# Other beginnings for the operands that TensorE streams, and two VectorE steps in another form

## The chip, the cores and the metric

One NeuronCore of a Trainium2 chip runs the kernel. The metric is the device time of one execution in microseconds; the time before is a median of 3 runs, and one more execution was profiled. Engines are named as in the profile: PE (TensorE matmul), PEld (its weight loads), DVE (VectorE), ACT (ScalarE), POOL (GpSimd), SP (SyncE, which issues the DMAs).

## The reference

Four batches of 12,416 rows of 128 go through an induced set attention with 32 inducing points, and the result through a gated feed-forward layer of 1536.

```python
def mab(q, kv):
    s = scale * (q @ kv.transpose(0, 2, 1))
    s = s - s.max(-1, keepdims=True)
    a = np.exp(s)
    a /= a.sum(-1, keepdims=True) + 1e-09
    return a @ kv
h = mab(I, x)
return mab(x, h).astype(np.float32)
...
g = x @ w_gate
silu = g * (1.0 / (1.0 + np.exp(-g)))
val = x @ w_val
return (silu * val @ w_out).astype(np.float32)
```

## The kernel before

The second attention is never written out. Its values `h` (32 rows) are multiplied into the two input weights of the feed-forward layer, which gives the tile `tw` for each batch. The attention weights of the rows, transposed and split into a rounded part and its rest (`a_hi`, `a_lo`, in the type fp32r), are copied by DMA into a tile `stack`, so that `tw` times `stack` is at once the gate and the value of the layer.

A batch has 25 column tiles: `COLS` lists one of the first four blocks (512 columns), then twelve of 16 blocks each (512 columns, numbers 1 to 12) and twelve of 15 blocks (480 columns, numbers 13 to 24). For each column tile the loop runs over 12 slices of the 1536 hidden units; one pass of it is a slot, 300 slots a batch. In a slot `front` issues two matmuls that stream `stack` (L668 gate, L669 value), ACT applies silu (L671), DVE multiplies (L676). One slot later `split` (from L679) makes `h_hi`, the product rounded to fp32r (L685, ACT or DVE), and `h_lo`, its rest (L687, POOL, or DVE for three of twelve slices). Five to ten slots after that (`SKEW`, `HI`), `back` issues three matmuls into one accumulator: `h_hi` with `wo_lo` (L701), `h_hi` with `wo_hi` (L702), `h_lo` with `wo_hi` (L703). After twelve slices DVE copies the accumulator out (L710) and SP stores it. The first column tile of the first batch is done in plain fp32 (L699) instead.

The operand that streams through PE is the second one here, of 512 or 480 columns; the weights are 128 columns of `tw`, `wo_hi` or `wo_lo`, loaded beside the matmul before. `stack` has three buffers, `h_hi` eleven, `h_lo` ten (`BF`, `NST`), each of 512 words a partition; gate and value share six PSUM buffers, two a tile.

The attention of the next batch is laid between the slots by due times (`plan`, `post`). For each group of blocks `post` issues: `sum2` (DVE: a sum, L441, and the addition of 1e-9, L442), `rec2` (DVE, L445), `norm2` (POOL, L449), `aT` (DVE transpose, L453), `a_hi` (DVE copy that rounds, L457; one of them, in the first batch, on ACT), `a_lo` (POOL, L462), and later `spread`, the DMAs into `stack`. Three short columns are made at the start on POOL: `odd`, `half`; a small tile `z` serves a short cut of the first batch only. `proj_c` (L397) is a correction matmul of the first batch that streams `tw` itself with the weights `below`; L385 is an fp32 matmul that makes `tw`.

The schedule is by hand (`tc.manual_schedule`), so the order of the code is the order on each engine. Pools lie in SBUF in the order in which they are opened.

Of the kernel before, what the change touches and what calls it, by code (L numbers as in the profile page):

```python
# [9 lines left out]
F32 = mybir.dt.float32  # L10
F32R = mybir.dt.float32r
AF = mybir.ActivationFunctionType
ALU = mybir.AluOpType
# [4 lines left out]
B, N, C, M, DFF = 4, 12416, 128, 32, 1536  # L18
P = 128
NG = 4  # L20
# [10 lines left out]
FC = [4, 16, 16, 16, 15, 15, 15]  # L31
FC0 = starts(FC)
NF = len(FC)
W = 32 * max(CH)
WF = 32 * max(FC)
NT = DFF // P
SCALE = 1.0 / math.sqrt(C)


COLS = [(0, 0)] + [(q, j) for q in range(1, NF) for j in range(NG)]  # L40
SLOTS = len(COLS) * NT
NXT = 4
# [66 lines left out]
def induced_set_attention_then_swiglu(ctx: ExitStack, tc: tile.TileContext, xt, xn, ind, wgv, wo, out):  # L109
    nc = tc.nc  # L110

    const = ctx.enter_context(tc.tile_pool(name="const", bufs=1))
    xtp = ctx.enter_context(tc.tile_pool(name="xtp", bufs=NXT))
    att = ctx.enter_context(tc.tile_pool(name="att", bufs=2))
    sgl = ctx.enter_context(tc.tile_pool(name="sgl", bufs=1))
    eTp = ctx.enter_context(tc.tile_pool(name="eTp", bufs=4))
    one = ctx.enter_context(tc.tile_pool(name="one", bufs=1))
    stp = ctx.enter_context(tc.tile_pool(name="stp", bufs=NST))
# [13 lines left out]
    group = const.tile([P, NG], F32, name="group")  # L132
    nc.vector.tensor_reduce(out=group, in_=ident.rearrange("p (j m) -> p j m", m=M), op=ALU.add, axis=AX.X)

    odd = const.tile([P, 1], F32, name="odd")
    nc.gpsimd.memset(odd, 0.0)
    for j in (1, 3):
        nc.gpsimd.memset(odd[32 * j:32 * j + 32, :], -1.0)


    half = const.tile([P, 1], F32, name="half")
    nc.gpsimd.memset(half[:64, :], 0.0)
    nc.gpsimd.memset(half[64:, :], -1.0)

    indT = const.tile([P, M], F32, name="indT")
    nc.sync.dma_start(out=indT, in_=ind)
# [15 lines left out]
    class Piece:  # L162
# [28 lines left out]

        def lo(self):
            nc.gpsimd.tensor_sub(out=wo_lo[:, self.cs], in0=self.w, in1=wo_hi[:, self.cs].bitcast(F32))

    class Batch:
        pass

    def attention(b, one, xn0=None, xt0=None):

        st = Batch()  # L200
# [216 lines left out]
        def sl2(b0, b1):  # L417
            return st.s2[:, b0:b1, :]
# [19 lines left out]
        def sum2(q):  # L438
            st.sm[q] = att.tile([P, 16], F32, name="sm")
            sm = st.sm[q][:, :FC[q]]  # L440
            nc.vector.tensor_reduce(out=sm, in_=sl2(*fblocks(q)), op=ALU.add, axis=AX.X)  # L441
            nc.vector.tensor_scalar(out=sm, in0=sm, scalar1=1e-9, scalar2=None, op0=ALU.add)  # L442

        def rec2(q):
            nc.vector.reciprocal(out=st.sm[q][:, :FC[q]], in_=st.sm[q][:, :FC[q]])  # L445
# [5 lines left out]
        def aT(q):  # L451
            st.at[q] = sgl.tile([P, WF], F32, name="aT")
            nc.vector.transpose(out=st.at[q][:, :32 * FC[q]], in_=sl2(*fblocks(q)).rearrange("p t m -> p (t m)"))  # L453

        def a_hi(q, eng=nc.vector.tensor_copy):
            st.ah[q] = sgl.tile([P, WF], F32R, name="a_hi")
            eng(out=st.ah[q][:, :32 * FC[q]], in_=st.at[q][:, :32 * FC[q]])  # L457

        def a_lo(q, eng):
            st.al[q] = sgl.tile([P, WF], F32R, name="a_lo")  # L460
            n = 32 * FC[q]
            eng.tensor_sub(out=st.al[q][:, :n], in0=st.at[q][:, :n], in1=st.ah[q][:, :n].bitcast(F32))  # L462

        def stack(u):
            if u not in st.stack:
                st.stack[u] = stp.tile([P, WF], F32R, name="stack")
            return st.stack[u]

        def spread(u):
# [19 lines left out]
            nc.vector.tensor_reduce(out=st.zm, in_=st.zps[:, :M * FC[0]].rearrange("p (t m) -> p t m", m=M), op=ALU.max, axis=AX.X)  # L489

        def z2():
            st.z = att.tile([P, FC[0], M], F32, name="z")
            nc.vector.tensor_sub(out=st.z, in0=st.zps[:, :M * FC[0]].rearrange("p (t m) -> p t m", m=M),
                                 in1=st.zm.unsqueeze(2).broadcast_to([P, FC[0], M]))

# [46 lines left out]
    def plan(st, p):  # L542
# [6 lines left out]
        def clear(slot):  # L549

            while slot % NT in p["TABU"]:
                slot += 1
# [50 lines left out]
    with tc.tile_pool(name="xt0", bufs=NCH - NXT) as xt0, tc.tile_pool(name="xn0", bufs=NCH - NXN) as xn0, tc.tile_pool(name="wtmp", bufs=1) as wtmp:  # L603
# [20 lines left out]
        def run(token):  # L624
# [17 lines left out]
            at=f["aT"], ah=lambda q, e=0: f["a_hi"](q, dve_act[e]),  # L642
# [8 lines left out]
    hip = ctx.enter_context(tc.tile_pool(name="hip", bufs=BF[2]))  # L651
    lop = ctx.enter_context(tc.tile_pool(name="lop", bufs=BF[3]))
# [5 lines left out]
    def front(st, b, c, t):  # L658
        u = Tile()
        q, j = COLS[c]  # L660
        u.b, u.q, u.j, u.t = b, q, j, t
        n = u.n = WF if q == 0 else 32 * FC[q]

        u.whole = b == 0 and c == 0
        rhs = st.stack[c][:, :n]
        u.g = ps_gv.tile([P, 512], F32, name="gv")
        u.v = ps_gv.tile([P, 512], F32, name="gv")
        nc.tensor.matmul(out=u.g[:, :n], lhsT=st.w[:, wcol(0, t)], rhs=rhs, start=True, stop=True)  # L668
        nc.tensor.matmul(out=u.v[:, :n], lhsT=st.w[:, wcol(1, t)], rhs=rhs, start=True, stop=True)  # L669
        s = sip.tile([P, WF], F32, name="silu")  # L670
        nc.scalar.activation(out=s[:, :n], in_=u.g[:, :n], func=AF.Silu)  # L671
        if u.whole:
            u.h = hip.tile([P, WF], F32, name="h_hi")
        else:
            u.h = u.v if t in DVE_TILES else hp.tile([P, WF], F32, name="h")
        nc.vector.tensor_mul(out=u.h[:, :n], in0=u.v[:, :n], in1=s[:, :n])  # L676
        return u

    def split(u):  # L679
        if u.whole:  # L680
            return
        n = u.n
        u.hi = hip.tile([P, WF], F32R, name="h_hi")
        u.lo = lop.tile([P, WF], F32R, name="h_lo")
        (nc.vector.tensor_copy if u.cast_dve else nc.scalar.copy)(out=u.hi[:, :n], in_=u.h[:, :n])  # L685
        eng = nc.vector if u.t in DVE_TILES or u.last else nc.gpsimd
        eng.tensor_sub(out=u.lo[:, :n], in0=u.h[:, :n], in1=u.hi[:, :n].bitcast(F32))  # L687
# [28 lines left out]
    for b in range(B):  # L716
# [12 lines left out]
        for slot in range(SLOTS):  # L729
            c, t = slot // NT, slot % NT  # L730
            u = front(cur, b, c, t)
# [62 lines left out]
```

## Time and profile before

| what | us |
|---|---|
| median of 3 runs | 1499.35 |
| lowest and highest of them | 1498.7, 1502.27 |
| the profiled execution | 1499.66 |
| its span, first to last instruction | 1497.6 |
| PE busy | 1475.7 |
| ACT, DVE, POOL busy | 1283.6, 1214.6, 1208.5 |

The profile is of one execution. The share of busy time says which engine has no room left; the chain of waits says what set the end; the table by stretch tells stages apart; the timeline gives single starts, to 0.01 us. A matmul's recorded length is longer than the distance to the next one's start, since matmuls are pipelined, so rates are read from starts.

### The profile page before, as it was taken

How to read it: one execution, taken by the hardware profiler on the slowest of the kernel's cores; microseconds unless marked ns; L12 is line 12 of the kernel's file. 1: busy time of each engine (PE TensorE's matmuls, PEld its weight loads, DVE VectorE, ACT ScalarE, POOL GpSimd, SP SyncE). 2: the span in 40 equal slices, each digit the busy share in tenths (PEclk: the TensorE clock that was granted, in tenths of full speed). 3: DMA queues.
4: the chain of work that ended last, by engine and by line, in shares of the span. 5: the costliest groups of instructions: out<-in, count | busy, mean ns of one | idle time of the engine just before them, and what ended most of it. 6: DMA issues, size and time to landing. Idle time of an engine off the chain costs nothing.

```text
span 1497.6 us, 24960 instructions
## 1 busy us (share of the span) xinstructions
PE 1475.7 (99%) x7465; PEld 1166.2 (78%) x7465; DVE 1214.6 (81%) x2083; ACT 1283.6 (86%) x2389; POOL 1208.5 (81%) x995
## 2 busy tenths in 40 slices
PE   8899999999999999999999999999999999999999
PEld 5576777788887776788887777678888887888887
DVE  6788778878888778788888878878878878878877
ACT  5787888789898887889989888789898898898897
POOL 1588767878898778788888877978889888888887
PEclk9999999999999999999999999999999999999999
DMA  9026322221133333121114324221111111111110
GB/s 369 23 94 187 135 96 94 79 61 56 40 109 120 122 125 112 46 67 37 40 44 131 125 87 156 78 69 48 41 40 35 38 41 41 33 41 39 41 40 20
DMA packets 50822, 119.80 MB, mean 80 GB/s; under 512 B 11392, under 2 KB 28288, under 8 KB 50688
## 3 DMA queue, kind: packets, MB, share of 16 engines
q1 hardware_dynamic: 50688, 118.22, 24.6%
q8 instruction: 59, 0.97, 0.3%
q14 instruction: 75, 0.61, 0.1%
HBM read 62.87 MB, written 25.43 MB: 59 GB/s over the span
## 4 chain that ended last, share of the span: by engine, by line
PE 87%; POOL 2%; ACT 2%; DVE 1%; issue 1%; DVEq 0%; ACTq 0%; POOLq 0%
PE o L701 17%; PE o L703 17%; PE o L702 16%; PE gv L668 16%; PE gv L669 16%; PE o L257 2%; POOL h_lo L687 2%; PE o L305 1%; ACT h_hi L685 1%; ACT silu L671 1%; POOL s_all L449 1%; DVE h L676 1%; PE gv L406 0%; ACT s_all L289 0%; DVE ob L710 0%
## 5 line engine op out<-in xcount | busy, mean ns | idle before, releaser
L687 POOL TENSOR_TENSOR h_lo<-h,h_hi 128x512 fp32r<-128x512 f32 (+1 forms) x890 | 1109.5, 1270 | 238.8 <-ACT h_hi L685 186.9
L671 ACT ACTIVATE silu<-gv 128x512 f32<-128x512 f32 (+1 forms) x1200 | 704.4, 588 | 127.0 <-PE gv L668 89.6
L676 DVE TENSOR_TENSOR h<-gv,silu 128x512 f32<-128x512 f32 (+1 forms) x891 | 594.3, 668 | 206.8 <-ACT silu L671 162.3
L685 ACT CAST h_hi<-h 128x512 fp32r<-128x512 f32 (+1 forms) x788 | 475.5, 603 | 54.0 <-DVE h L676 47.6
L668 PE MATMUL gv<-stack,tw 128*128 128x512 f32 (+1 forms) x1200 | 469.3, 391 | 1.3 <-ACT h_hi L685 0.8
L701 PE MATMUL o<-h_hi,wo_lo 128*128 128x512 f32 (+1 forms) x1188 | 464.4, 391 | 3.8 <-DVE ob L710 2.1
L703 PE MATMUL o<-h_lo,wo_hi 128*128 128x512 f32 (+1 forms) x1188 | 463.2, 390 | 0.6
L669 PE MATMUL gv<-stack,tw 128*128 128x512 f32 (+1 forms) x1200 | 461.8, 385 | 1.8 <-DVE h L676 0.6
L702 PE MATMUL o<-h_hi,wo_hi 128*128 128x512 f32 (+1 forms) x1188 | 458.5, 386 | 0.0
L701 PEld LDWEIGHTS o<-h_hi,wo_lo 128*128 128x128 f32 x1188 | 223.0, 188 | 81.9 <-issue 33.9
L669 PEld LDWEIGHTS gv<-stack,tw 128*128 128x128 f32 x1200 | 225.2, 188 | 53.9 <-ACT silu L671 4.8
L668 PEld LDWEIGHTS gv<-stack,tw 128*128 128x128 f32 x1200 | 225.7, 188 | 50.2 <-issue 3.8
L703 PEld LDWEIGHTS o<-h_lo,wo_hi 128*128 128x128 f32 x1188 | 222.4, 187 | 52.6 <-POOL h_lo L687 12.1
L702 PEld LDWEIGHTS o<-h_hi,wo_hi 128*128 128x128 f32 x1188 | 223.2, 188 | 36.8
L676 DVE TENSOR_TENSOR gv<-gv,silu 128x512 f32<-128x512 f32 (+1 forms) x297 | 201.7, 679 | 46.4 <-ACT silu L671 40.7
L687 DVE TENSOR_TENSOR h_lo<-gv,h_hi 128x512 fp32r<-128x512 f32 (+1 forms) x297 | 197.3, 664 | 1.0
L685 ACT CAST h_hi<-gv 128x512 fp32r<-128x512 f32 (+1 forms) x294 | 167.9, 571 | 4.8 <-DVE gv L676 2.5
L710 DVE COPY ob<-o 128x512 f32<-128x512 f32 (+1 forms) x100 | 66.3, 663 | 1.4 <-PE o L703 1.4
L685 DVE CAST h_hi<-h 128x512 fp32r<-128x512 f32 (+1 forms) x103 | 46.1, 448 | 0.0
L462 POOL TENSOR_TENSOR a_lo<-aT,a_hi 128x512 fp32r<-128x512 f32 (+2 forms) x27 | 36.2, 1340 | 1.5 <-ACT a_hi L457 1.5
L433 POOL TENSOR_TENSOR s_all<-s_all,mx 128x448 f32<-128x448 f32 (+3 forms) x28 | 26.9, 961 | 0.7 <-DVE mx L429 0.7
L449 POOL TENSOR_TENSOR s_all<-s_all,sm 128x512 f32<-128x512 f32 (+2 forms) x27 | 25.9, 958 | 0.4 <-DVE sm L445 0.4
(159 smaller groups left out, 497.4 us busy)
## 6 DMA issues: line engine op xcount, KB each, us to landing
xt_sb<-xt SPq DMA_DIRECT2D x32, 896.0 KB, 5.1
xn_sb<-xn SPq DMA_DIRECT2D x18, 896.0 KB, 6.2
out<-ob SPq DMA_DIRECT2D x52, 256.0 KB, 2.0
out<-ob SPq DMA_DIRECT2D x48, 240.0 KB, 2.0
stack<-a_hi SPq DMA_DIRECT2D x96, 64.0 KB, 2.0
stack<-a_lo SPq DMA_DIRECT2D x96, 64.0 KB, 2.0
stack<-a_hi SPq DMA_DIRECT2D x96, 60.0 KB, 2.0
stack<-a_lo SPq DMA_DIRECT2D x96, 60.0 KB, 2.0
```

What stands on the lines that cost most here:

```text
L449: eng.tensor_mul(out=a, in0=a, in1=st.sm[q][:, :FC[q]].unsqueeze(2).broadcast_to([P, FC[q], M]))
L462: eng.tensor_sub(out=st.al[q][:, :n], in0=st.at[q][:, :n], in1=st.ah[q][:, :n].bitcast(F32))
L668: nc.tensor.matmul(out=u.g[:, :n], lhsT=st.w[:, wcol(0, t)], rhs=rhs, start=True, stop=True)
L669: nc.tensor.matmul(out=u.v[:, :n], lhsT=st.w[:, wcol(1, t)], rhs=rhs, start=True, stop=True)
L671: nc.scalar.activation(out=s[:, :n], in_=u.g[:, :n], func=AF.Silu)
L676: nc.vector.tensor_mul(out=u.h[:, :n], in0=u.v[:, :n], in1=s[:, :n])
L685: (nc.vector.tensor_copy if u.cast_dve else nc.scalar.copy)(out=u.hi[:, :n], in_=u.h[:, :n])
L687: eng.tensor_sub(out=u.lo[:, :n], in0=u.h[:, :n], in1=u.hi[:, :n].bitcast(F32))
L701: nc.tensor.matmul(out=o[:, :n], lhsT=wo_lo[:, ws], rhs=u.hi[:, :n], start=(t == 0), stop=False)
L702: nc.tensor.matmul(out=o[:, :n], lhsT=wo_hi[:, ws], rhs=u.hi[:, :n], start=False, stop=False)
L703: nc.tensor.matmul(out=o[:, :n], lhsT=wo_hi[:, ws], rhs=u.lo[:, :n], start=False, stop=(t == NT - 1))
L710: nc.vector.tensor_copy(out=ob[:, :n], in_=o[:, :n])
```

## The change

Four things change. The buffers of `stack`, `h_hi` and `h_lo` become 64 words longer, and the operand inside begins some words further on: by 16, 48 and 48 words (`stack`, `h_hi`, `h_lo`) in column tiles 0 to 12, by 0, 32 and 16 words in tiles 13 to 24. `a_hi` on DVE becomes the maximum of a tile with itself. The constant 1e-9 is added from a column of SBUF, repeated along the row, and not as an immediate number. `odd`, `half` and the new column share one tile, and `z` moves to a pool with one buffer.

```diff
 WF = 32 * max(FC)
+WB = WF + 64
+AT = (16, 48, 48), (0, 32, 16)
...
-    odd = const.tile([P, 1], F32, name="odd")
+    marks = const.tile([P, 16], F32, name="marks")
+    odd, half, eps = marks[:, 0:1], marks[:, 1:2], marks[:, 2:3]
...
-    half = const.tile([P, 1], F32, name="half")
     nc.gpsimd.memset(half[:64, :], 0.0)
     nc.gpsimd.memset(half[64:, :], -1.0)
+    nc.gpsimd.memset(eps, 1e-9)
...
+    def at(u):
+
+        return AT[u > NG * FC.count(max(FC))]
...
-            nc.vector.tensor_scalar(out=sm, in0=sm, scalar1=1e-9, scalar2=None, op0=ALU.add)
+            nc.vector.tensor_add(out=sm, in0=sm, in1=eps.broadcast_to([P, FC[q]]))
...
-        def a_hi(q, eng=nc.vector.tensor_copy):
+        def a_hi(q, eng=lambda out, in_: nc.vector.tensor_max(out=out, in0=in_, in1=in_)):
...
-                st.stack[u] = stp.tile([P, WF], F32R, name="stack")
+                st.stack[u] = stp.tile([P, WB], F32R, name="stack")[:, at(u)[0]:][:, :WF]
...
-            st.z = att.tile([P, FC[0], M], F32, name="z")
+            st.z = sgl.tile([P, FC[0], M], F32, name="z")
...
+        u.at = at(c)
...
-            u.h = hip.tile([P, WF], F32, name="h_hi")
+            u.h = hip.tile([P, WB], F32, name="h_hi")[:, :WF]
...
-        u.hi = hip.tile([P, WF], F32R, name="h_hi")
-        u.lo = lop.tile([P, WF], F32R, name="h_lo")
+        u.hi = hip.tile([P, WB], F32R, name="h_hi")[:, u.at[1]:u.at[1] + WF]
+        u.lo = lop.tile([P, WB], F32R, name="h_lo")[:, u.at[2]:u.at[2] + WF]
```

The change's own name calls the new beginnings 224, and 160, 160, 96.

## Rows read from the trace of the kernel before

**Rows 1.** The page, part 1: busy us, share of the span, instructions.
```profile
PE 1475.7 (99%) x7465; PEld 1166.2 (78%) x7465; DVE 1214.6 (81%) x2083; ACT 1283.6 (86%) x2389; POOL 1208.5 (81%) x995
```
**Rows 2.** The page, part 4: the chain that ended last, shares by engine.
```profile
PE 87%; POOL 2%; ACT 2%; DVE 1%; issue 1%; DVEq 0%; ACTq 0%; POOLq 0%
```
**Rows 3.** Busy time by stretch: PE, PEld, DVE, ACT, POOL, clock, DMA.
```profile
1200.00:1400.00 200.00, 199.91 (x883) 164.29 (x882) 163.89 (x266) 180.87 (x340) 174.36 (x141) 1.00 0.13 39
```
**Rows 4.** Timeline of PE: start us, length us, what; two stretches, their ends.
```profile
1204.34 0.39 PE L668 MATMUL gv<-stack,tw 128*128 128x512 f32 x1
1204.57 0.39 PE L669 MATMUL gv<-stack,tw 128*128 128x512 f32 x1
1204.80 0.39 PE L701 MATMUL o<-h_hi,wo_lo 128*128 128x512 f32 x1
1205.03 0.39 PE L702 MATMUL o<-h_hi,wo_hi 128*128 128x512 f32 x1
...
1243.33 0.39 PE L668 MATMUL gv<-stack,tw 128*128 128x512 f32 x1
...
1086.96 0.38 PE L668 MATMUL gv<-stack,tw 128*128 128x480 f32 x1
...
1134.48 0.38 PE L668 MATMUL gv<-stack,tw 128*128 128x480 f32 x1
```
**Rows 5.** Groups of PE by line within the two stretches of rows 4.
```profile
L669 PE MATMUL gv<-stack,tw 128*128 128x512 f32 x34 | 13.2, 388 | 0.0
...
L669 PE MATMUL gv<-stack,tw 128*128 128x480 f32 x44 | 16.6, 377 | 0.0
```
**Rows 6.** Groups by line and shape, whole span: busy us, mean ns, idle before.
```profile
L669 PE MATMUL gv<-stack,tw 128*128 128x512 f32 x624 | 244.1, 391 | 1.8 <-DVE h L676 0.6 <-DVE h_hi L676 0.6 <-ACT silu L671 0.4
L703 PE MATMUL o<-h_lo,wo_hi 128*128 128x512 f32 x612 | 242.2, 396 | 0.0
L703 PE MATMUL o<-h_lo,wo_hi 128*128 128x480 f32 x576 | 221.0, 384 | 0.6
```
**Rows 7.** L699 in fp32: timeline of one matmul's two passes; their group.
```profile
50.53 1.02 PE L699 MATMUL o<-h_hi,s_all 128*128 128x512 f32 x2
...
L699 PE MATMUL o<-h_hi,s_all 128*128 128x512 f32 x2 | 1.0, 592 | 0.0
```
**Rows 8.** Timeline of PE around L397, which streams `tw`.
```profile
51.85 0.39 PE L397 MATMUL gv<-tw,below 128*128 128x512 f32 x1
52.09 0.40 PE L668 MATMUL gv<-stack,tw 128*128 128x512 f32 x1
...
52.56 0.67 PE L385 MATMUL gv<-wgv_sb,hT 128*128 128x512 f32 x1
```
**Rows 9.** DVE instructions of three lines: ns min/median/max, first and last start us.
```profile
L457 DVE CAST a_hi<-aT x26: 291/1098/1525, 103.3 to 1411.6; 128x480 fp32r<-128x480 f32 x12, 128x512 fp32r<-128x512 f32 x11, 128x128 fp32r<-128x128 f32 x3
...
L685 DVE CAST h_hi<-h x103: 399/416/1478, 80.3 to 1491.4; 128x512 fp32r<-128x512 f32 x55, 128x480 fp32r<-128x480 f32 x48
...
L442 DVE TENSOR_SCALAR sm<-sm x27: 169/989/1090, 53.6 to 1404.5; 128x16 f32<-128x16 f32 x12, 128x15 f32<-128x15 f32 x12, 128x4 f32<-128x4 f32 x3
```
**Rows 10.** L184 alone (its group), and in the timeline beside POOL.
```profile
L184 DVE SCALAR_TENSOR_TENSOR work<-work x2: 693/693/693, 28.2 to 31.4; 128x512 uint32<-128x512 uint32 x2
...
57.32 1.32 POOL L462 TENSOR_TENSOR a_lo<-aT,a_hi 128x512 fp32r<-128x512 f32 x1 [1.48 <-ACT a_hi L457]
57.53 1.65 DVE L184 SCALAR_TENSOR_TENSOR xn_sb<-xn_sb 128x512 uint32<-128x512 uint32 x1
```
**Rows 11.** The page, part 5: POOL's two steps for each group of blocks.
```profile
L462 POOL TENSOR_TENSOR a_lo<-aT,a_hi 128x512 fp32r<-128x512 f32 (+2 forms) x27 | 36.2, 1340 | 1.5 <-ACT a_hi L457 1.5
...
L449 POOL TENSOR_TENSOR s_all<-s_all,sm 128x512 f32<-128x512 f32 (+2 forms) x27 | 25.9, 958 | 0.4 <-DVE sm L445 0.4
```
**Rows 12.** Waits of PE's weight loads: us in total, times, longest.
```profile
PEld o L703 <- POOL h_lo L687: 12.1, 39, 0.5
```

## The prediction

> **What bounds the kernel now.** I read the busy table first, to see which engine has no room: PE is busy for 1475.7 of 1497.6 us, while DVE and POOL stand at 81% [rows 1]. Busy alone proves little on a pipelined engine, so the chain of waits comes next: 87% of it is PE, 2% POOL, 1% DVE [rows 2]. The table by stretch says the same of a late stage: from 1200 to 1400 us PE lacks 0.09 of 200 us, at the full clock of 2.4 GHz (granted 1.00) [rows 3]. So in the long middle the time is the number of matmuls times the distance from one start to the next, and a change counts there only through that distance or by making PE wait.
>
> The distance comes from the timeline. In a stretch of 512-column matmuls with nothing between, L668 starts at 1204.34 and again at 1243.33 us [rows 4]; between lie 34 slots of five matmuls [rows 5], so 38.99 us / 170 = 229.4 ns. In a 480-column stretch it is from 1086.96 to 1134.48 us, 44 slots: 47.52 / 220 = 216.0 ns. At 2.4 GHz the columns alone take 512 / 2.4 = 213.3 and 480 / 2.4 = 200.0 ns. **Beyond its columns a matmul pays 16 ns, the same in both widths.** There are 2 x 624 + 3 x 612 = 3084 matmuls of 512 columns and 5 x 576 = 2880 of 480 [rows 6]: 5964 x 16 ns = 95 us. This is the pot from which the change could draw, or to which it could add.
>
> **Part 1: the beginnings.** The diff shifts the tile that PE streams (the moving operand: `stack`, `h_hi`, `h_lo`) inside a buffer lengthened by 64 words. The change's name gives the new beginnings modulo 256 bytes: 224 for all three in 512-column tiles, and 160, 160, 96 in 480-column tiles. The shifts in `AT` are 64, 192, 192 and 0, 128, 64 bytes; subtracted, they leave buffers at 160 (`stack`) and 32 (`h_hi`, `h_lo`). All that the change adds ahead of them (64 bytes where two tiles of 32 were; `z` once instead of twice; 256 bytes a buffer) is zero or a multiple of 256, so before it the operands began at 160, 32, 32 in both widths. The weights `tw`, `wo_hi`, `wo_lo` begin at 224 throughout, by the order and size of the tiles ahead of them. Modulo 256, `stack` stood 64 bytes below its weights, and `h_hi` and `h_lo` 64 above. After the change all 512-column operands stand level with theirs; of the 480-column ones `stack` doesn't move, `h_hi` goes from 64 above to 64 below, `h_lo` to 128 away.
>
> No instruction is added or removed; only the 16 ns can change. Does that part depend on where a read begins? For: an fp32 matmul of L699, two passes of 512 columns at half rate, lasts 592 ns a pass and 1.02 us for both, so its passes start 0.428 us apart [rows 7]; 1024 columns' time is 426.7 ns, so it pays 1.3 ns, with the same weight load beside it. The other 14.7 ns thus belong to the full-rate stream, and two streams that read memory together could meet more or less often as their beginnings stand. Against: the steps from L668 to L669 (160, 64 below the weights) and from L701 to L702 (32, 64 above) are both 0.23 us [rows 4], and the 16 ns are the same in two widths whose tiles end at different places.
>
> The Trainium skill, "TensorE: Matmul & The Clock Gate", section "Step-by-step: what each phase is for", says that PE has two independent read ports and that loading the next weights takes no read bandwidth from the running matmul. By that rule the beginnings are worth nothing and the sum below stands; the trace has 14.7 ns that the rule doesn't explain, so I don't lean on it.
>
> The level position has one near witness: L397 streams `tw`, which begins at 224, with the next weights from 224 behind it. From its start at 51.85 to that of L385 at 52.56 us are three steps [rows 8], 0.237 us each, among them two of operands that begin at 160. That is 7.3 ns over 229.4, but at the start of the kernel, where other things disturb PE. The bounds for a 512-column matmul are therefore -14.7 ns (all that L699 doesn't pay) and +7.3 ns: 3084 x -14.7 = -45 us and 3084 x 7.3 = +23 us. For 480 columns `h_hi` goes to where `stack` already is (0), and `h_lo` is 576 matmuls, -8 to +4 us. I take 0 for both widths: the rows nearest to it are the plain steps of operands that stand 64 bytes below and above the weights, which are alike to the 10 ns that the timeline shows.
>
> **Part 2: `a_hi` by a maximum.** 26 copies on DVE (L457) become `tensor_max` of a tile with itself; the one on ACT stays. They last 291 to 1525 ns, median 1098 [rows 9]; a cast of the same kind that isn't held takes 416 ns (median of L685) [rows 9], so most of a copy is waiting. For what? The pair that shows it is L184, a DVE instruction with two operands in SBUF: 693 ns alone, but 1.65 us where POOL's `a_lo` runs from 57.32 to 58.64 us; it ended 0.54 us after POOL did [rows 10]. So a DVE instruction with two operands from SBUF stands still while POOL reads there, and then takes its full 0.54 us. `tensor_max` is of that kind: it would still wait, and afterwards take 693 - 416 = 277 ns longer than a copy, 23 times in the wide form and a quarter of it 3 times in the narrow: 6.6 us more of DVE, and as much more hold on POOL's next instruction. What reaches PE? POOL's extra work for the attention (L449 25.9 us, L462 36.2 us, [rows 11]) now makes PE wait 12.1 us for `h_lo` [rows 12]: 12.1 / 62.1 = 0.19. So 0.19 x 6.6 = **+1.3 us**. Bounds: +6.6 us if all of it reaches PE; if the maximum doesn't wait, a copy's 1098 become 693 ns and POOL is held no more: taken as the mirror image, -1.3 us.
>
> The Trainium skill, "SBUF — State Buffer", section "Who interferes with whom", has the same rule: a DVE instruction with two SBUF inputs contends with a GpSimd instruction that reads SBUF, as does a copy in its two-port mode. By it parts 2 and 3 don't free DVE. L184's 1.65 us agrees.
>
> **Part 3: the softmax constant from a column.** 27 instructions (L442) change from `tensor_scalar` to an add of two operands. They last 169 to 1090 ns, median 989 [rows 9], for 16 elements: 0.82 us of waiting. With two operands in SBUF they wait as before: **0**. If they didn't, DVE would gain 27 x 0.82 = 22 us, all of it covered now: the multiply (L676) queued behind it frees the PSUM pair that L668 needs three slots later (six buffers, two a tile), 3 x 1.08 us, and what it makes is read five slots later (`SKEW`), so of a wait of 0.8 us nothing reaches PE; without that cover it would be the 22 us. I take 0, bounds 0 and -2 us (0.19 of half of it, through POOL).
>
> **Part 4: the rest.** `odd`, `half`, `eps` share a tile: one more memset before the first load is used. `z` runs once, in the first batch, so one buffer waits for nobody. The buffers of the main loop lie up to 5.6 KB further on, over tiles of the start that are long read. 0, give or take 1 us.
>
> **Sum.** On the profiled execution's own 1499.66 us (span 1497.6 plus 2.06 around it): 0 + 1.3 + 0 + 0 = 1501.0 us. That execution is 0.31 us over the median of 1499.35, so the forecast is about **1500.5 us**, no change within what can be told (0.3% is 4.5 us).
>
> **Rivals.** *Faster: the reads meet less often.* If standing level spares a quarter to a half of the 14.7 ns, the 512-column matmuls give 3084 x 3.7 = 11 us to 3084 x 7.3 = 23 us: 1478 to 1489 us. For it: L699's 1.3 ns says that the 16 ns aren't a law of loading weights. Against: the two beginnings seen differ by nothing. *Slower: they meet more often.* Two reads from level beginnings start on the same place at once; L397's stretch speaks for it. At a third of its 7.3 ns, 3084 x 2.4 = +7.5 us: 1508 us. It decides from 1.5 ns per 512-column matmul on. *Slower by POOL:* all of part 2 reaches PE, 1506 us; against it, PE hardly waits in [rows 3]. *The change doesn't do what it says:* the maximum and the column add don't get out of POOL's way; that is in the forecast, and if they do, it is 1497 us, still no change.
>
> **How the numbers follow.** No change 0.39; faster by the beginnings 0.37; slower by the beginnings 0.20, by POOL 0.04. The two ends of part 1 are open, and a rate paid 5964 times makes 1 ns worth 6 us, so the range goes to 1480 below (the deep end of the faster case left out) and to 1510 above (the whole of L397's 7.3 ns left out). Within 0.3%: 0.39; faster 0.37; slower 0.24.
>
> **What would show it.** The distance between starts in a pure 512-column stretch: 229.4 ns if part 1 is right, under 227.9 or over 230.9 if a rival is; for 480 columns 216.0. L457 as a maximum: a median near 1.37 us if it still waits, 0.69 if not; L442's successor near 1 us or near 0.17. POOL's `h_lo` on the chain at 2% or more. Wrong would be: a 512-column distance that moves while the 480-column one stands still, or PE waits for `h_lo` well away from 12 us.

## The result, and the profile after

The changed kernel takes 1506.31 us (median of 16 runs, 1501.46 to 1511.66) beside 1499.66 us for the one before, run alongside it (16 runs, 1498.52 to 1502.32). The ratio is 1.0041 with a 95% interval of 1.0032 to 1.0049: **slower by 6.65 us**, more than the 0.3% that the prediction named as the limit of what can be told. 1500.5 us was forecast; the time lies inside the range of 1480 to 1510, but the likeliest case, no change, did not come. The range was that wide for other reasons (the open price of the beginnings), so that 1506.31 us lies in it is in part luck. The profiled execution took 1506.9 us with a span of 1504.9, 7.3 us over the span of before (1497.6).

Parts 1 and 4 of the page after: busy us, share and instructions of each engine, and the chain that ended last.

```profile
PE 1478.1 (98%) x7465; PEld 1166.1 (77%) x7465; DVE 1226.9 (82%) x2083; ACT 1281.1 (85%) x2389; POOL 1218.9 (81%) x996
...
PE 76%; POOL 8%; issue 4%; ACT 3%; DVE 2%; DMA 0%; SPq 0%; POOLq 0%; DVEq 0%; ACTq 0%
```

Beside [rows 1], DVE and POOL are busy 12.3 and 10.4 us longer. Beside [rows 2], POOL's share of the chain went from 2% to 8%, where `h_lo` (L687 before, L695 now) is 7%. PE is busy only 2.4 us longer, so a good part of the 7.3 us is waiting (a matmul's recorded length is modelled; the sum from starts stands below). Lines have moved: the five matmuls of a step, L668, L669 and L701 to L703 before, are now L676, L677 and L709 to L711; the maximum is L462, the column add L449.

**The beginnings.** The distance between starts, read as in [rows 4, 5]: timeline of PE, first start and last of a stretch with nothing between; then the count of L676 from the first start to just ahead of the last.

```profile
1209.59 0.40 PE L676 MATMUL gv<-stack,tw 128*128 128x512 f32 x1
1250.40 0.39 PE L676 MATMUL gv<-stack,tw 128*128 128x512 f32 x1
...
357.08 0.38 PE L676 MATMUL gv<-stack,tw 128*128 128x480 f32 x1
409.55 0.38 PE L676 MATMUL gv<-stack,tw 128*128 128x480 f32 x1
...
319.36 0.38 PE L676 MATMUL gv<-stack,tw 128*128 128x480 f32 x1
341.90 0.38 PE L676 MATMUL gv<-stack,tw 128*128 128x480 f32 x1
```

```profile
L676 PE MATMUL gv<-stack,tw 128*128 128x512 f32 x36 | 14.0, 389 | 0.0
...
L676 PE MATMUL gv<-stack,tw 128*128 128x480 f32 x48 | 18.4, 384 | 0.0
...
L676 PE MATMUL gv<-stack,tw 128*128 128x480 f32 x21 | 8.0, 380 | 0.0
```

With 512 columns it is 40.81 us / 180 = **226.7 ns**, 2.7 ns less than before. With 480 columns there is no longer one distance: 52.47 / 240 = **218.6 ns** in one stretch, 22.54 / 105 = **214.7 ns** in another, where before it was 216.0 in 427 of 500 undisturbed steps of five (worked out from all starts). Both widths moved, in opposite directions, and neither was forecast to.

**The maximum and the column add.** Instructions of three lines (ns min / median / max, first and last start, forms), and two of PE's waits (us in total, times, longest):

```profile
L462 DVE TENSOR_TENSOR a_hi<-aT x26: 357/1360/2600, 103.0 to 1417.8; 128x480 fp32r<-128x480 f32 x12, 128x512 fp32r<-128x512 f32 x11, 128x128 fp32r<-128x128 f32 x3
L449 DVE TENSOR_TENSOR sm<-sm,marks x27: 161/1041/1099, 53.3 to 1410.6; 128x16 f32<-128x16 f32 x12, 128x15 f32<-128x15 f32 x12, 128x4 f32<-128x4 f32 x3
L695 POOL TENSOR_TENSOR h_lo<-h,h_hi x890: 1214/1294/1782, 64.8 to 1498.4; 128x512 fp32r<-128x512 f32 x91, 128x480 fp32r<-128x480 f32 x87
```

```profile
PEld o L711 <- POOL h_lo L695: 15.7, 39, 0.6
...
PE gv L676 <- DVE h L684: 2.5, 5, 1.0
```

The maximum's median of 1360 ns answers to 1098 in [rows 9], the add's 1041 to 989. PE's loads wait 15.7 us for `h_lo` where [rows 12] has 12.1, in as many waits (39), so the same waits have become longer.

**Where the 7.3 us are.** The next table is worked out from the starts of all PE matmuls of 480 and 512 columns in the two traces: what a step from one start to the next takes beyond the columns at 2.4 GHz, summed apart for plain steps (under 30 ns beyond) and for longer gaps (less 16 ns each).

```
us              512: plain   gaps     480: plain   gaps
before               47.1    23.1          45.7     6.5
after                41.5    25.4          49.2    11.8
difference           -5.6    +2.3          +3.5    +5.3     all else +1.4
```

The 512-column steps gave back 5.6 us. The plain 480-column steps took 3.5 of it again, and the waits took 7.6 us. Where the waits are shows when the starts of the gate matmul are set beside before step by step: behind the first 125 us the distance grows by 0.25 to 0.36 us at 16 places, each behind a maximum, 4.6 us in all, and by 1.1 us at two more, 2.2 us, which are shown below.

### The profile page after: what moved, and what is told of

Read it like the earlier page. It is cut to its first block, busy times and chain, and to the rows that moved or that the text cites. A ratio compares the mean times of both kernels' runs of the same rounds, so it can differ in the third digit from the quotient of the medians.

```text
span 1504.9 us, 24961 instructions
## 1 busy us (share of the span) xinstructions
PE 1478.1 (98%) x7465; PEld 1166.1 (77%) x7465; DVE 1226.9 (82%) x2083; ACT 1281.1 (85%) x2389; POOL 1218.9 (81%) x996
## 4 chain that ended last, share of the span: by engine, by line
PE 76%; POOL 8%; issue 4%; ACT 3%; DVE 2%; DMA 0%; SPq 0%; POOLq 0%; DVEq 0%; ACTq 0%
PE o L709 15%; PE o L711 14%; PE gv L676 14%; PE gv L677 14%; PE o L710 14%; POOL h_lo L695 7%; PE o L264 2%; DVE h L684 1%; PE o L312 1%; ACT silu L679 1%; ACT h_hi L693 1%; POOL s_all L456 1%; POOL a_lo L469 0%; PE gv L413 0%; DMA stack<-a_lo 0%
## 5 line engine op out<-in xcount | busy, mean ns | idle before, releaser
L695 POOL TENSOR_TENSOR h_lo<-h,h_hi 128x512 fp32r<-128x512 f32 (+1 forms) x890 | 1120.9, 1285 | 236.0 <-ACT h_hi L693 181.9
L684 DVE TENSOR_TENSOR h<-gv,silu 128x512 f32<-128x512 f32 (+1 forms) x891 | 594.3, 668 | 201.8 <-ACT silu L679 136.2
L676 PE MATMUL gv<-stack,tw 128*128 128x512 f32 (+1 forms) x1200 | 470.8, 392 | 3.9 <-DVE h L684 2.5
L709 PE MATMUL o<-h_hi,wo_lo 128*128 128x512 f32 (+1 forms) x1188 | 465.4, 392 | 4.9 <-DVE ob L718 3.2
L677 PE MATMUL gv<-stack,tw 128*128 128x512 f32 (+1 forms) x1200 | 463.7, 386 | 2.2 <-DVE h L684 0.9
L711 PE MATMUL o<-h_lo,wo_hi 128*128 128x512 f32 (+1 forms) x1188 | 461.8, 389 | 1.9 <-POOL h_lo L695 0.3
L709 PEld LDWEIGHTS o<-h_hi,wo_lo 128*128 128x128 f32 x1188 | 222.6, 187 | 83.7 <-issue 33.9
L711 PEld LDWEIGHTS o<-h_lo,wo_hi 128*128 128x128 f32 x1188 | 223.0, 188 | 56.7 <-POOL h_lo L695 15.7
L677 PEld LDWEIGHTS gv<-stack,tw 128*128 128x128 f32 x1200 | 225.7, 188 | 51.9 <-ACT silu L679 6.0
L676 PEld LDWEIGHTS gv<-stack,tw 128*128 128x128 f32 x1200 | 225.3, 188 | 51.7 <-DVE h L684 6.2
L684 DVE TENSOR_TENSOR gv<-gv,silu 128x512 f32<-128x512 f32 (+1 forms) x297 | 201.7, 679 | 46.2 <-ACT silu L679 40.6
L695 DVE TENSOR_TENSOR h_lo<-gv,h_hi 128x512 fp32r<-128x512 f32 (+1 forms) x297 | 197.6, 665 | 1.2
L718 DVE COPY ob<-o 128x512 f32<-128x512 f32 (+1 forms) x100 | 66.4, 664 | 1.4 <-PE o L711 1.4
L693 DVE CAST h_hi<-h 128x512 fp32r<-128x512 f32 (+1 forms) x103 | 49.8, 484 | 0.0
L462 DVE TENSOR_TENSOR a_hi<-aT 128x480 fp32r<-128x480 f32 (+2 forms) x26 | 33.1, 1273 | 0.0
```

The lines of the kernel that those rows point to most:

```text
L462: def a_hi(q, eng=lambda out, in_: nc.vector.tensor_max(out=out, in0=in_, in1=in_)):
L709: nc.tensor.matmul(out=o[:, :n], lhsT=wo_lo[:, ws], rhs=u.hi[:, :n], start=(t == 0), stop=False)
L711: nc.tensor.matmul(out=o[:, :n], lhsT=wo_hi[:, ws], rhs=u.lo[:, :n], start=False, stop=(t == NT - 1))
L718: nc.vector.tensor_copy(out=ob[:, :n], in_=o[:, :n])
```

## The experiments

Three theories stood for the 6.65 us. **POOL:** the maxima hold POOL's `h_lo`, and PE pays; the beginnings are worth little in sum. **The beginnings:** those at 480 columns cost what the run shows, and the maxima are covered. **The layout:** the longer buffers and the shared tile of constants do it. In the expectations the first is theory H and the second theory B; theory M, from the fifth experiment on, says that the 480-column matmuls keep one of several paces until something disturbs PE. All edits are against the changed kernel unless the text says otherwise. Each kernel's median is set beside that of the kernel before, run alongside it.

**The beginnings alone** (copy and immediate constant restored):

```diff
-            nc.vector.tensor_add(out=sm, in0=sm, in1=eps.broadcast_to([P, FC[q]]))
+            nc.vector.tensor_scalar(out=sm, in0=sm, scalar1=1e-9, scalar2=None, op0=ALU.add)
...
-        def a_hi(q, eng=lambda out, in_: nc.vector.tensor_max(out=out, in0=in_, in1=in_)):
+        def a_hi(q, eng=nc.vector.tensor_copy):
```

> The new beginnings alone: the maximum and the column add are taken back to the copy and the immediate. Theory H (the maximum holds DVE and POOL longer and PE waits for it; the beginnings take about as much from the 512-column matmuls as they give to the 480-column ones): 1497 to 1500 us against 1499.7 of the kernel before, i.e. a ratio of 0.998 to 1.000, with the distances of the changed kernel (512 columns 226.7 ns, 480 columns 218.7 ns for most) and PE's lost time outside the plain steps back near that of before. Theory B (the beginnings alone cost it, by the 480-column distance and by a POOL that runs h_lo 6 to 10 ns slower): 1505 to 1507 us, ratio about 1.004.

1506.57 us (1501.21 to 1515.56, 11 runs), ratio 1.0041 [1.0026, 1.0057]. The beginnings alone are as slow as the whole change, which speaks for the beginnings; but the profiled run is the fastest of the eleven (1501.21 us), so its trace doesn't show what the slower ones lost. Its chain has POOL at 1%, and covers only some 70% of the span.

**The two DVE edits alone** (all beginnings where they were):

```diff
-AT = (16, 48, 48), (0, 32, 16)
+AT = (0, 0, 0), (0, 0, 0)
```

> The two DVE edits alone: the buffers stay 64 words longer, but all operands begin where they did before. Theory H: 1504 to 1508 us, ratio 1.003 to 1.006, distances 229.4 and 216.0 ns as before. Theory B: 1499 to 1501 us, ratio 1.000, and POOL's h_lo at 1299 and 1232 ns median as before.

1506.86 us (1504.62 to 1507.65, 5 runs), 1.0040 [1.0027, 1.0054]. These alone are as slow as the whole, too. So neither POOL nor the beginnings can be the whole cause by itself: the parts don't add up.

**The maximum alone** (beginnings where they were, constant as an immediate):

> The maximum alone, without the column add and with the old beginnings. Theory H puts all of the loss on the maximum: the same time as with both DVE edits, 1504 to 1508 us. If the column add carries part of it, this run stands below that one by that part. Theory B: 1499 to 1501 us.

1504.80 us (1501.62 to 1507.42, 10 runs), 1.0032 [1.0021, 1.0043]: **+4.0 us**. In its trace little else moves behind the first 125 us, so one place can be followed. DVE, POOL and PE's waiting load in the timeline, first in the kernel before, then in this one (start us, length us, instruction, idle before it and what ended it):

```profile
411.88 1.17 DVE L457 CAST a_hi<-aT 128x512 fp32r<-128x512 f32 x1
...
415.51 1.46 POOL L462 TENSOR_TENSOR a_lo<-aT,a_hi 128x512 fp32r<-128x512 f32 x1
416.93 4.79 POOL L687 TENSOR_TENSOR h_lo<-h,h_hi 128x480 fp32r<-128x480 f32 x4
...
418.21 0.19 PEld L703 LDWEIGHTS o<-h_lo,wo_hi 128*128 128x128 f32 x1 [0.32 <-POOL h_lo L687]
```

```profile
410.46 1.42 DVE L462 TENSOR_TENSOR a_hi<-aT 128x512 fp32r<-128x512 f32 x1
...
414.34 1.47 POOL L469 TENSOR_TENSOR a_lo<-aT,a_hi 128x512 fp32r<-128x512 f32 x1
415.77 4.77 POOL L695 TENSOR_TENSOR h_lo<-h,h_hi 128x480 fp32r<-128x480 f32 x4
...
417.04 0.19 PEld L711 LDWEIGHTS o<-h_lo,wo_hi 128*128 128x128 f32 x1 [0.56 <-POOL h_lo L695]
```

The maximum is 0.25 us longer than the copy (1.42 to 1.17). The `h_lo` behind `a_lo` starts 5.31 us after it began, beside 5.05, and the load that waits for it waits 0.24 us longer (0.56 to 0.32). Nothing is hidden here, since PE was already waiting at this point. The delay reaches POOL by two ways of the same length: POOL's `h_lo` beside the maximum are held (four take 5.23 us, 4.97 before), and the multiply queued behind the maximum on DVE comes later, and with it the `h_hi` for which POOL waits next (0.18 us, 0.19 before). Set beside before step by step, the distance between two starts of the gate matmul grows so at 17 places of the run, by 0.19 to 0.29 us each, 4.2 us in all, and hardly anywhere else but in the first 125 us. That is the size of the +4.0 us by which the median is longer (the traced run itself, the fastest of the ten, is only 1.8 us over before in its span, since it was some 2 us ahead at 125 us); the other 9 of the 26 maxima are covered. The trace of both DVE edits has the same places, 16 of them behind 130 us with 3.8 us.

**The beginnings at 512 alone:**

```diff
-AT = (16, 48, 48), (0, 32, 16)
+AT = (16, 48, 48), (0, 0, 0)
```

with copy and immediate restored.

> Beginnings of the 512-column operands moved to 224, the 480-column ones left at 160, 32, 32, no DVE edit. If a distance belongs to its own beginnings alone: 226.7 ns for 512 columns and 216.0 for 480, some 2.7 ns less for about 3000 matmuls: 1499.7 - 8 = 1492 us, ratio 0.995; theory H expects this or a little more. Theory B, by which POOL pays for shifted operands, expects 1495 to 1500 us.

1503.18 us (1497.31 to 1509.28, 12 runs), 1.0019 [1.0005, 1.0034]. PE in the timeline, two ends of a 512-column stretch (38 steps of five by the count of L676) and of a 480-column one (65):

```profile
1205.34 0.40 PE L676 MATMUL gv<-stack,tw 128*128 128x512 f32 x1
1248.42 0.39 PE L676 MATMUL gv<-stack,tw 128*128 128x512 f32 x1
...
1421.72 0.38 PE L676 MATMUL gv<-stack,tw 128*128 128x480 f32 x1
1491.94 0.38 PE L676 MATMUL gv<-stack,tw 128*128 128x480 f32 x1
```

43.08 / 190 = 226.7 ns and 70.22 / 325 = 216.1 ns: the gain at 512 columns belongs to these beginnings, and the 480-column steps are as before. The gain of some 5.6 us doesn't reach the time. Part of where it goes is in the trace: a copy of `a_hi` at 596.46 us lasted 2.67 us, and its column of tiles takes 2.1 us longer than before; and PE waited 2.5 us for a transfer of `stack` ahead of 126.66 us, as it did in the trace after (1.4 us) and in that of the buffers alone (2.1 us), so that this isn't of the beginnings. Behind that wait the granted clock was lower for a while. PE in the timeline, and its busy time by stretch with the clock (0.57 here, 1.00 in the same stretch before; the two levels are 2.4 and 1.2 GHz):

```profile
126.66 0.47 PE L676 MATMUL gv<-stack,tw 128*128 128x512 f32 x1 [2.50 <-DMA stack<-a_lo]
...
127.00:131.00 4.00, 4.00 (x15) 0.57 0.28 41
```

**Only the longer buffers and shared constants** (no shift, copy and immediate):

> The longer buffers alone: 64 words more each, every operand at its old beginning modulo 256 bytes, the copy and the immediate as before. Theory H and theory M (it is the beginnings modulo 256 and the maximum that act) both expect the time of before, 1499 to 1502 us, with 229.4 and 216.0 ns. If the lengthening itself costs (other addresses modulo 512, other neighbours), 1503 us and more, and the runs with the old beginnings and the DVE edits owe that much to it.

1500.04 us (1498.23 to 1502.43, 11 runs), 1.0003 [0.9994, 1.0013]. The layout is out. Its distances are 229.4 and 216.0 ns as before (medians of steps of five, from all starts), though each buffer has moved by a multiple of 256 bytes.

**The beginnings at 480 alone:**

```diff
-AT = (16, 48, 48), (0, 32, 16)
+AT = (0, 0, 0), (0, 32, 16)
```

with copy and immediate restored.

> Only the 480-column operands get the new beginnings (160, 160, 96), the 512-column ones stay. Theory M: the 480-column matmuls sit either at 1093 ns or at 1073 ns for a slot's five (before: 1080) and stay there until something disturbs PE, so the time goes up to 576 x 13 ns = 7.5 us above or 576 x 7 = 4 us below the 1500.8 of before, from one execution to the next: runs from 1496 to 1509 us, median near 1506, where the run with all beginnings stood. If the 480-column beginnings don't matter for the median, 1500 to 1502 us.

1505.43 us (1502.86 to 1508.93, 5 runs), 1.0039 [1.0026, 1.0052]: **+6.1 us**. PE in the timeline, the two ends of three 480-column stretches (50, 50 and 23 steps of five) and a 512-column one (38):

```profile
357.70 0.38 PE L676 MATMUL gv<-stack,tw 128*128 128x480 f32 x1
412.04 0.38 PE L676 MATMUL gv<-stack,tw 128*128 128x480 f32 x1
...
1087.30 0.37 PE L676 MATMUL gv<-stack,tw 128*128 128x480 f32 x1
1141.94 0.39 PE L676 MATMUL gv<-stack,tw 128*128 128x480 f32 x1
...
320.28 0.38 PE L676 MATMUL gv<-stack,tw 128*128 128x480 f32 x1
344.97 0.38 PE L676 MATMUL gv<-stack,tw 128*128 128x480 f32 x1
...
1208.47 0.39 PE L676 MATMUL gv<-stack,tw 128*128 128x512 f32 x1
1252.05 0.40 PE L676 MATMUL gv<-stack,tw 128*128 128x512 f32 x1
```

54.34 / 250 = 217.4 ns, 54.64 / 250 = 218.6 ns, 24.69 / 115 = 214.7 ns, and 43.58 / 190 = 229.4 ns. So at these beginnings PE has at least three paces for the same five matmuls, keeps one for tens of steps, and mostly changes it behind a disturbance. Of the undisturbed steps of five at 480 columns (worked out from all starts), 271 of 503 in this trace stand at 218.6 ns a matmul and 77 at 214.7; in the trace after it is 301 and 92 of 499, in that of the beginnings alone 198 and 226 of 505. Of the three, the last has the most steps at the fast pace and is the shortest (1501.21 us).

**Four more sets of beginnings, in turn by column:**

```diff
-AT = (16, 48, 48), (0, 32, 16)
+AT = (32, 0, 0), (48, 16, 16), (0, 32, 32), (16, 48, 48)
...
-        return AT[u > NG * FC.count(max(FC))]
+        return AT[u % 4]
```

with copy and immediate restored.

> A map of beginnings in one execution: column tile u takes one beginning for stack, h_hi and h_lo alike, 32, 96, 160 or 224 modulo 256 bytes for u modulo 4 = 0, 1, 2, 3, in both widths; no DVE edit. Theory M expects the distance to follow the position relative to the weights' 224: level (224) 226.7 ns for 512 columns as measured, 64 above and 64 below (32, 160) 229.4 ns, and the untried 96 either; for 480 columns 216.0 ns at 32 and 160, and another value at 96 and 224. If every uniform set has the same distance, the gain at 512 came from all three operands beginning alike, and 226.7 ns stands in all four.

1509.22 us in one run. It was meant as a map: one trace with all three operands level at 32, 96, 160 and 224 bytes, in both widths. It settles little: next to a change of beginnings the steps fall into a slow pace, so that at 512 columns even the set that gives 226.7 ns elsewhere shows 230.6 in most of its steps (medians of steps of five, from all starts). What a set is worth when it stands alone can't be read from this trace.

**The kernel before, with `a_hi` on ACT instead of DVE:**

```diff
-        def a_hi(q, eng=nc.vector.tensor_copy):
+        def a_hi(q, eng=nc.scalar.copy):
```

> The kernel before with all 26 copies a_hi moved from DVE to ACT, nothing else. Theory H (a_hi costs through the port that DVE and POOL share): POOL's a_lo goes from 1429 and 1404 ns towards 1300 and 1232, no h_lo is held, and PE's 12.1 us of waiting for h_lo falls by 2 to 4 us; but ACT gets 26 x 0.6 us more, so 1496 to 1501 us. If the loss with the maximum came from DVE's own length and not from holding POOL, PE's wait for h_lo stays at 12 us.

1500.10 us (1497.93 to 1503.9, 11 runs), 1.0003 [0.9995, 1.0012]. Its step (the groups by form; ns min / median / max), POOL's, and PE's wait:

```profile
L457 ACT CAST a_hi<-aT x27: 299/592/621, 55.3 to 1409.9; 128x512 fp32r<-128x512 f32 x12, 128x480 fp32r<-128x480 f32 x12, 128x128 fp32r<-128x128 f32 x3
...
L687 POOL TENSOR_TENSOR h_lo<-h,h_hi x890: 1207/1281/1351, 63.7 to 1489.6; 128x512 fp32r<-128x512 f32 x91, 128x480 fp32r<-128x480 f32 x87
...
PEld o L703 <- POOL h_lo L687: 13.5, 39, 0.5
```

On ACT the step takes 592 ns and holds no `h_lo`: the longest falls from 1492 ns before to 1351. That PE waits no less for `h_lo` (13.5 us, [rows 12] has 12.1) speaks against the copy's hold having set that wait before; ahead of it stands `a_lo` [rows 11], as in the place shown above. It doesn't prove it, since ACT, which makes most of `h_hi`, got the step's time in exchange.

**The column add alone:**

> The column add alone (longer buffers, old beginnings, the copy for a_hi). The forecast had put it at 0: it waits for POOL as the immediate did. So 1499 to 1502 us, 27 instructions of L442's successor at a median near 1 us. If it costs, the run with both DVE edits (6 us slower) stood above that with the maximum alone (4 us) because of it, and this one comes out near 1502 to 1503 us.

1500.69 us (1498.02 to 1503.7, 11 runs), 1.0004 [0.9994, 1.0014]. Its median instruction is 986 ns beside 989 in [rows 9]. It waits as it did, and costs nothing that can be told.

**Two maxima in a row** (the same result computed twice; otherwise the maximum alone):

```diff
-        def a_hi(q, eng=lambda out, in_: nc.vector.tensor_max(out=out, in0=in_, in1=in_)):
+        def a_hi(q, eng=lambda out, in_: [nc.vector.tensor_max(out=out, in0=in_, in1=in_) for _ in range(2)]):
```

> The suspected cost doubled: a_hi by two maxima, one after the other, with the old beginnings and the immediate. Theory H, by which each maximum holds DVE and POOL and PE waits 0.2 to 0.3 us for it: the second maximum adds 0.7 us of DVE to 26 places; with the share seen for the first one (4 us for 6.6 us of longer DVE) 26 x 0.69 x 0.6 = 11 us more, so 1511 to 1517 us. If PE's loss doesn't grow with the length of a_hi but belongs to something else in that run, 1504 to 1506 us.

1539.83 us (1539.37 to 1540.89, 4 runs), 1.0270 [1.0255, 1.0286]: +40 us, far over what was expected. Its maxima and PE's waits:

```profile
L462 DVE TENSOR_TENSOR a_hi<-aT x52: 293/1427/1806, 103.5 to 1451.0; 128x480 fp32r<-128x480 f32 x24, 128x512 fp32r<-128x512 f32 x22, 128x128 fp32r<-128x128 f32 x6
```

```profile
PEld gv L677 <- DVE h L684: 28.4, 22, 2.9
PEld o L711 <- POOL h_lo L695: 18.0, 39, 0.8
...
PE gv L677 <- DVE h L684: 19.1, 17, 2.6
```

The expectation added the instruction's own time. But each of the two waits anew for a POOL instruction to end, so DVE stands for some 2.8 us, and then the multiply queued behind it frees its PSUM buffers too late: the wait that grows is that for `h` (`L677`'s loads waited 2.5 us in the trace of the maximum alone), while that for `h_lo` goes from 15.2 to 18.0 us. That fits the cover that Part 3 of the prediction named, three steps of 1.08 us: one such wait stays under it, two in a row use it up.

**The changed kernel and the beginnings at 512, once more each:**

> The changed kernel once more, unchanged, for a second trace of the same program. Theory M: the 480-column slots again stand at 1093, 1087 or 1073 ns, but the share of each differs from the first trace (1093 in 301 of 499), and the time goes with the share: more at 1093, later end. If the shares are the same to a few slots, the spread of the runs has another source.

> The kernel with the 512-column beginnings alone once more, for a second trace. Theory M: where its runs come out at 1503 and not at 1494 us, either many 512-column slots stand at 1154 instead of 1133 ns (42 of 454 in the first trace), or a_hi is passed over by a second POOL instruction in several places (4 in the first trace), each costing PE about 1 to 2 us. If neither shows, the lost 8 us stay open.

1507.97 us and 1497.84 us. The first has 236 of 506 undisturbed 480-column steps at 218.6 ns and 150 at 214.7, another split than the 301 and 92 of the first trace: the same program takes up its paces differently from run to run. The second has 226.7 ns at 512 columns again, with a span of 1495.9 us, 1.7 us under that of before; the same copy as in the first trace is held there (2.68 us at 592.42 us), but PE doesn't wait for `stack` near 125 us.

**Set beside before by stretch.** How much later or earlier than before the gate matmul starts, by the number of the step (36 starts at 93.8 us and 108 at 190.0 us in the trace of before; worked out from starts, one trace each):

```
us against before          to 36   36 to 108   108 to the last
after                       -0.5     +1.1        +6.6
after, second trace         +1.4     +0.2        +6.6
both DVE edits              +0.2     +3.5        +4.2
maximum alone               -1.5     -0.4        +3.7
column add alone            -0.4     -0.8        -0.1
buffers alone               -0.6     +2.8        +0.1
beginnings alone            -0.4     +3.3        -1.4
512 alone                   -0.3     +3.3        -0.6
512 alone, second trace     -0.6     -0.5        -0.6
480 alone                   -0.1     +2.4        +6.7
```

In the middle stretch five traces of this table lose 2.4 to 3.5 us, the buffers alone among them. All five waited 1.8 to 2.8 us for `stack` there, and behind it the granted clock from 127 to 131 us was 0.57 to 0.66; in the others that wait is 1.4 us or missing and the clock 1.00. So this loss isn't of one edit; an execution has it or not, and a median may hold it. Behind step 108 the rows are plainer: the layout and the add cost nothing, the maximum 3.7 to 4.2 us, the 512-column beginnings give 0.6 us twice, and the change costs 6.6 us twice. There the second trace of the change paid in another way than the first: one maximum, at 595.56 us, lasted 2.92 us, and PE then waited 3.1 us for the accumulator's copy (L718), which stood behind that maximum on DVE; behind that the granted clock was 0.57 from 600 to 604 us.

## Where the prediction was right and where it was wrong, point by point

**What bounds the kernel: right.** All that moved the time in the traces did so through the distance between starts, by making PE wait, or by the lower granted clock behind such a wait, which the prediction didn't count.

**Part 1, 0 for both widths: wrong, one of the two steps that failed.** The prediction took 0 because two positions, 64 bytes below the weights and 64 above, were alike. From that it doesn't follow that a third is alike too. Standing level at 224 gives 226.7 ns instead of 229.4, -2.7 ns inside the bounds of -14.7 to +7.3. The direction is that of the rival "faster", the size is less than its lower end (3.7 ns). L397's 7.3 ns, the one witness for "level is slower", had the sign the wrong way; where its 7.3 ns came from no run shows. For 480 columns "`h_hi` goes to where `stack` already is" was no ground for 0: the pace goes from 216.0 to 218.6, 217.4 or 214.7 ns. In plain steps both widths sum to -5.6 + 3.5 = -2.1 us, near the forecast's 0 only because they cancel: luck, and of that trace, since the share of each pace differs from run to run.

The Trainium skill, "TensorE: Matmul & The Clock Gate", section "Step-by-step: what each phase is for", says that loading weights takes no read bandwidth from the running matmul. Here the same five matmuls with the same loads beside them step by 229.4 or 226.7 ns when only the beginnings of the moving operands differ. So the beginnings are worth something, and the prediction's reading of that rule, by which they are worth nothing, doesn't hold. Whether it is the loads that meet the stream isn't shown, so no run here decides on the rule itself.

**Part 2, +1.3 us: the mechanism right, the size wrong, the other step that failed.** The median of about 1.37 us was forecast and 1.36 us came (1.33 in the maximum alone). What failed is the share that reaches PE. 12.1 / 62.1 = 0.19 was an average over all of POOL's extra work, wherever it lies. The maximum lengthens the same chain, though, at a place where PE is already waiting for its end (39 waits of 0.3 us on average), so behind that point its price is paid whole: 0.24 of 0.25 us in the place shown, 4.2 us in all, of 6.0 us by which the 26 instructions grew (6.6 were forecast): a share of 0.70. "PE hardly waits in [rows 3]" was likewise a mean over 200 us. In the trace after it is 4.6 us at the 16 places, and the two places shown below on top. The rival "slower by POOL" had the mechanism, but as a bound: at 6.6 us it charged every maximum in full; it was given 0.04.

**Part 3, 0: right.** 1.0004 for the add alone, and it waits as before. The cover named for it fits the experiment with two maxima.

**Part 4, 0: right.** 1.0003 for the buffers alone.

**What the sum missed: the beginnings change when things meet.** In the trace after, two of the maxima were held by two POOL instructions and not by one. The timeline of DVE, POOL and PE there (start us, length us):

```profile
345.22 3.62 POOL L695 TENSOR_TENSOR h_lo<-h,h_hi 128x480 fp32r<-128x480 f32 x3
...
346.78 2.58 DVE L462 TENSOR_TENSOR a_hi<-aT 128x480 fp32r<-128x480 f32 x1
347.78 0.38 PE L676 MATMUL gv<-stack,tw 128*128 128x480 f32 x1
349.28 0.65 DVE L684 TENSOR_TENSOR h<-gv,silu 128x480 f32<-128x480 f32 x1
349.98 0.48 PE L676 MATMUL gv<-stack,tw 128*128 128x480 f32 x1 [0.96 <-DVE h L684]
```

The maximum outlasts the `h_lo` that it met and the next one, too, and ends 0.51 us after that; the multiply L684 comes 2.50 us after the maximum began, and the next gate matmul starts 2.20 us after the last instead of 1.08. At the same place of the kernel before, the copy at 346.47 us took 1.10 us. That POOL runs back to back doesn't set the two cases apart, since it does so in the ordinary ones, too. There DVE's instruction ends behind the first `h_lo` that it met, and it is the next one that is held. POOL in the timeline, the `h_lo` that the maximum met and the next, merged: at the place shown above for the maximum alone, then here.

```profile
410.11 2.87 POOL L695 TENSOR_TENSOR h_lo<-h,h_hi 128x480 fp32r<-128x480 f32 x2
...
346.40 2.44 POOL L695 TENSOR_TENSOR h_lo<-h,h_hi 128x480 fp32r<-128x480 f32 x2
```

What decides whether DVE or POOL's next goes first isn't shown. In the trace after this happens at 346.78 and 1077.76 us, and each time that column of tiles takes 1.5 us longer than before, beside 0.2 us in the maximum alone. It happens to the plain copy, too, in traces with other beginnings: to 2.33 us twice in the beginnings at 480 alone, to between 2.1 and 2.7 us four times in those at 512 alone. In the trace of before the longest copy is 1525 ns [rows 9].

**The rivals.** None came as told. "Faster" was right in direction at 512 columns and was eaten; "slower by POOL" was right in kind; "slower by the beginnings" gave 1508 us, next to the 1506.31 that came, but for the wrong width: luck. "The change doesn't do what it says" was in the forecast and holds: neither the maximum nor the add gets out of POOL's way. Of the signs named ahead, a 512-column distance under 227.9 ns came; the 480-column one didn't stand still beside it, as the sign had it; and the waits for `h_lo` went from 12.1 to 15.7 us.

**What stays open.** Why PE keeps one of several paces at the 480-column beginnings and what makes it choose: the traces show the paces, not their cause. Why the kernel with the 512-column beginnings has its median at 1503.18 us: its first trace, at 1501.75 us, lost 3.3 us in the stretch from 94 to 190 us and the second, at 1497.84, didn't, but no run above 1502 us was traced. And the parts don't add up: the medians beside before are +4.0 (maximum), +1.3 (add), +6.1 (480) and +2.4 (512), 13.8 us together, and the whole is +6.65. Part of it may go with the clock: the runs' mean granted clock differs, 0.994 to 0.999 for the beginnings alone and 0.997 to 1.000 for the kernel before beside them. At 0.998 alone the former has four runs of 1501.21 to 1508.66 us, the latter eight of 1499.11 to 1502.62, so a difference and a wider spread remain. Waits that share a place, and paces that are chosen anew after each disturbance, would make the rest; it is only argued here. No version of several runs had a median under that of the kernel before.

## What to carry to other kernels

A share of waiting that is averaged over a whole run says little of an edit at one place: look there for an engine that is already waiting for the end of the chain that the edit lengthens, and charge the whole price if there is one. Where a rate is paid thousands of times, "two positions are alike" is no evidence on a third; a change of addresses has to be run, at each width by itself. An engine that waits for another's instruction to end can be passed over by the next one, too, so such a wait can double without its own instruction having changed. And where a few microseconds are at stake, set two traces beside each other by stretch: a loss that a version without the edit has in the same stretch, too, isn't the edit's.

## What the runs showed of the hardware

- The distance between matmuls of an fp32r operand depends on where the operand begins in its partition: for 512 columns 229.4 ns at 160, 32, 32 and 226.7 ns at 224 (bytes modulo 256, with weights at 224). Buffers moved by multiples of 256 bytes alone kept 229.4 ns.
- It needn't be one number: for 480 columns at 160, 160, 96 it was 218.6, 217.4 or 214.7 ns, each kept over tens of steps, and two traces of the same kernel had the slowest in 301 of 499 and in 236 of 506 undisturbed steps.
- A DVE instruction with two operands in SBUF that meets a running one of POOL's `h_lo` waits for it to end, and so does a rounding copy: in 480 and 512 columns the maximum ended 0.51 to 0.55 us after a POOL instruction, the copy 0.26 to 0.29 us (medians of their whole length 1.36 and 1.10 us). Where a second POOL instruction went first, the maximum took 2.58 and 2.60 us. The Trainium skill, "SBUF — State Buffer", section "Who interferes with whom", has this contention, and the trace agrees with it.
